# Token weights of a spectral mixer: transposed on TensorE in place of the DMA, with a new instruction order

## Chip, cores and metric

The kernel runs on one core of a Trainium2 chip. The metric is the device time of one execution in microseconds. Engines are named as in the profile: PE is TensorE (PEld its weight loads), DVE is VectorE, ACT is ScalarE, POOL is GpSimd, SP is the engine that issues all DMAs here.

## What is computed

Two stages follow each other for a batch of 4, sequence length 768. The first is attention of 8 heads of width 64 that looks only at selected chunks of 32 keys: an upper bound of each chunk's scores is formed from the minimum and maximum of its keys, and the six chunks with the highest bound are kept. The second mixes tokens and channels with a phase.

```python
ub = sum(maximum(q * k_min, q * k_max))            # per query and chunk
top_chunks = argsort(where(causal, ub, -1e9))[..., -6:]
scores = where(selected & causal, q @ k.T / 8, -1e9)
x = softmax(scores) @ v                            # heads joined: (4, 768, 512)

theta = x @ w_theta
zr, zi = x * cos(theta), x * sin(theta)
y = einsum('ts,bsd->btd', w_tok_r, zr) + einsum('ts,bsd->btd', w_tok_i, zi)
u = x + y
out = u + maximum(u @ w_ch, 0)
```

All inputs and the output are fp32; the kernel computes its large products in fp16 with fp32 accumulation.

## The kernel before

**Attention.** Heads are worked in pairs, four pairs in each batch. `Lk`, `Lq` and `Lv` load a pair's keys, queries and values. PE turns keys and queries (`Tk`, `Tq`, L230 for batch 0 and L433 for the others), ACT and DVE bring them from PSUM to SBUF as `kx` and `qT` (L169 is ACT's copy helper, L171 DVE's, L172 POOL's), and DVE reduces the keys to the minima and maxima of the chunks (`km`, L239 and L445). PE forms the bounds (`ub`, L277 and L482), DVE finds each query's sixth largest and makes a mask of it, which is copied into extra rows of the queries (L526). Scores `sc` come from L341/L349 or L554, ACT exponentiates them (L357, L560), POOL or DVE cut the triangle (L369, L570, L568), PE multiplies with the values (`av`, L401), and DVE normalizes into `x16` (L411, L412).

**Mixer.** For each batch: `x16` is transposed (`xT`, by PE at L598 with copies at L582/L583, or by DMA at L590 for batches 2 and 3), `th` (L608) gives theta, ACT takes sine and cosine (L615, L619), DVE or POOL form `zi` and `zr` (L623). For each of six tiles of 128 output tokens, twelve matmuls of 512 columns (L633, L635) accumulate `y`, with the transposed token weights `K.wtok` as the stationary operand; DVE adds x (`u`, L641). `u` is transposed (by DMA at L647 or PE at L654), multiplied with `w_ch` (`ch`, L662), and `ot` (L668) goes out by L672.

**Token weights.** `weights()` brings the two 768x768 matrices in 12 row blocks, named by `ri` (real or imaginary) and `tt` (six blocks of 128 rows). Each block is loaded (`Lwtok`, L697) into one of six buffers of class `ld`, cast to fp16 (`cwtok`, on ACT, DVE or POOL) into one of four buffers of class `st`, and transposed into `K.wtok` by a DMA that SP issues (`Twtok`, L702). The tile `t` of every batch's mixer needs the two blocks with `tt = t`.

**Order.** The program is first recorded as a list of operations (`op` for one engine, `alt` for several engines to choose from), each with a cost in ns that only an offline search used. A string `ORDER` fixes the order in which all of them are issued and, by a suffix `b` or `c`, the second or third alternative for the engine. Each engine runs its own instructions in that order, and buffers of a class are handed out in that order too. A number before the bar in the string is a count of idle matmuls of 512 columns at the start that keep PE running, and an entry `F5` is five of 128 columns.

**Buffers that matter here.** PSUM has two tiles of class `sc` of two banks each, one of class `av` and three of class `mi`; the last serves turns, bounds, theta, y and ch.

Of the kernel before, what the change touches and what calls it, by code (L numbers as in the profile page):

```python
# [11 lines left out]
FP16 = mybir.dt.float16  # L12
# [6 lines left out]
    "4 1 2 29 477b 380b 730b 3 28 31 30 0 21 58 5 57 9 476 10 F5 14 6 17 55 15 7 406 36 18 12b 16 32 20b 56 8b "  # L19
    "19 39 11 48 34 13b F19 41 33 44 42 85 23 37 45 75 38 47b 35b 40b 24 22 50 25 450 26 82 51 F10 71 27 68 83 "  # L20
    "52 72 176 109 173 177 69b 167 178 174 84 53 59 74 63 168 379 61 175 161 65 162 64 164 169 60 113 165 54 "
    "F6 170 163 67b 179 46 62b 66 77 166 171 43c 49c 202 76c 199 102 203 78 172 185 134 200 193 204 79 184 194 "
    "183 201 90 186 187 110 190 91 188 195 181 92 125 95 80 98 191 96b 189 196 115 114 81 86 99 93b 192 376 "
    "180 73b 70 87 209 197 375 88 225 401 103c 101b 402 213 198b 377 211 226 94 182 135 210 378 104 212 214 "
    "227 136 126 89b 228 105 222 215 229 106 265 127 116 223 219 230 207 107 266b 381 224 403 108 216 404 384 "
    "220 206 111 385 100 205 131 386 217 97 208 412 221 242 140 390 414 218 413 254 388b 233 255 231 405 389 "
    "232 243 256 239 416 391b 415 240 248 244 234 237 236 249 387b 241 235 245 238 383 267 250 246 251 268 407 "
    "451 729 252 269 247 410 128 411 270b 258 253 259 417b 257 409 112c 262 132 408 260 261 137 263 382 392 "
    "264 394 133 141 393 395 271 418 398b 397 272 142 420 396b 419b 278 129c 123 421b 138 283 280 130 423 298 "
    "424 139 293 299 282 300 273 301 149 295 119 427 152 274 124 158 275 276 146 428 284 155 437 288 294 277 "  # L30
    "279 286b 303 302 285 281b 310 289 297 304 287 150b 311 291b 296b 312 290 151 429 120 305 438 430 153b 317 "
    "318 292 422b 154 439 319 159b 320 431 321 440 147b 121 432 322 160 441 306 434c 323 307 442b 445c 444b "
    "308 443c 148 156b 436c 562 309 530 433c 563 349 435 313 157 331 332 122 333 117 531 564 543 143 314 399 "
    "350b 334 532 449 544 517 425 345 448 335 346 518 470 559 545b 338 560 519 339 118 340 341 561 447 144c "
    "342 446 315 145 549 316 343 550 556 400c 472 363 344 551 557 475 533 364 474 355 534 336 558b 356 347 546 "
    "337 348b 372 535b 547 365 357 373 473 426b 548 523 358 536 524 554 553 552 471b 353 525b 374 555 520 537 "
    "465 354 463 727 521 466b 538 540 457 452 726 464 461 522 539 469b 541 467 459b 324 453 542 325 728 458 "
    "326 456 327 359 460 526 527 455 496 328 454b 462b 329 468c 528 753 489 330 369 490 754 529 483 370 725 "
    "621 484 566 622b 371 565 486 567 478 485b 491 480 751 487 492 481 351 752 495b 494 360 482 479b 488b 749 "
    "493 352 742 361 366 743 568 362 498 367 497b 368 623 508 624 797 744 509 768 499 745 510 796 769 766 747 "  # L40
    "736 746b 767b 731 773 511 738 735 770 772b 795 512 733 739 514c 732 794 740 516c 513b 760 771b 515c 737b "
    "585 818 763 611 586 764 755 748 612 759 750 588 819 757b 587 762 734 608 821 589 613b 500 741b 820 758 "
    "761 582 590 609 501 765b 816 775 502 583 610 503 505c 506b 507b 584 756 774 601 785 776 504c 595 1070 602 "
    "786 777 1069 787 592 596 603 572 778 811 591 573 597 569 779 798 788 812 803 574 801 575 570 1068 827 780 "
    "593 1067 807 784c 576 598 594 783c 829 614 577 789 599 571 580 831 793c 579 830 615 792c 578 890 600 806 "
    "828 906 616 581 800 618 782c 907 617 790c 802 619 604 804 605 620 908 606 805 808b 887 799 607 822 891 "
    "625 817c 840 627 626 888 1089 893 628 1071 826 894 654 889 1073b 824 895 1074 903 823 791 656 898 825 900 "
    "1072b 634 832b 892b 781 1075 841 896 897 655 629 658 635 1091 657b 636 1092 899 639 637 630 644 631 638 "
    "632b 641 649 633 640 1090c 646 643 666 1134 642b 667 645 1135 648 668 651 647b 687 650 653 688 904 652 "
    "689 669 659 660 661 901 662 905b 663 690 902 670 909 664 877 665 691 878 867 701 692 868 911 879 880 693 "  # L50
    "910 881 869 861 705 912 671 862 882 874 672 809 875 833 863 810b 1113 835 864 702 834b 836 885 876b 815b "
    "707 813c 865 837c 1156 884 839 883 708 838 719 886 709 866 842 720 1114b 814c 871 721 872 852 1158 870 "
    "673 843 1159 674 853 873 680 681 854 1076 1157c 682 1077 1180 855 683 1078 1094 844 856 684 1093 845 685 "
    "858b 859c 857b 675 686 860b 932 958 846 933 1095 704 1079 676 1096 847 934 929 1097 1080 848c 677 959 "
    "1098 850c 678 930 1081b 1099 926 960 679 1100 927 1084 931 1101b 1137 1082 955 703 849 1083 851 928b 937 "
    "1085 1102b 916 956 1103 1086 716 1136 1104 1160 917 1087 935 1161 913 717 1108 957 914 1106 718 918 919 "
    "1105 1088 710 1109 1107b 915 920 1112 942 711 1110 936 943 1115 938 712 921 1111 694 1116 952 944 1125 "
    "1143 1117 953 1126 713 1118 1127 1144 939 1145 923 954b 940 945 1128 924 1119 695 1129 946 696 941 1146 "
    "697 1133c 1131b 1120 947 698 714 1124b 1132c 699 1123b 1122c 1147 922 715 1230 1121c 700 1240 1130c 1231 "
    "925 1151 706 1138 1152b 1162 1241 1232 1246 1139b 948 962 1141 1247 1242 1233 1164b 949 1140 1248 1243 "  # L60
    "1166 1234 961 1142 963 1244 950 1235 1227 964 1167 951 1228 1207 1245 1149 1170 1250 968 1208 1229 1171 "
    "1214 1150 1249 1148 1169b 1209 1204 1215 1154 969 1165 1175 1251 1163b 1168 1153 1201 1252 1205 966 1173 "
    "1216 722 1174b 1176 1172 1202 1206b 965 1237 1179 1236 723 1178 1238 1217 1177b 1239 1220 1203 724 991 "
    "1218 967 1155 1181c 1182 1221 1219 970 993 1222 1224 1192 1225 1223 1183 976 1226 992 971 1184 995 978 "
    "994b 1212 1185 977 981 973 980 1210 1186 972 1211 975 996 982 979b 974b 983 986 984b 998 1193 985 1187 "
    "1008 997 1000b 1194 1009 987 1015 988 1213 999 1016 1190b 1017 1191b 1010 1188b 990b 1022 1285 1279 1189c "
    "1286 1023 989b 1024 1195 1018 1196 1019 1200 1197c 1280 1011 1287 1259 1020 1198b 1281 1253 1260 1021 "
    "1025 1199b 1261 1256 1254 1045 1012 1001 1257 1255 1292 1002 1293 1258 1269 1263 1270 1264 1294 1282 1003 "
    "1283 1271 1262 1026 1265 1266 1284 1295 1267 1290 1289 1027 1296 1268 1272 1028 1288 1013 1273 1291 1297 "
    "1298 1046 1036 1299 1274b 1037 1014 1277 1300 1275 1276 1044 1301 1303 1278 1302 1004 1304 1005 1006 1309 "  # L70
    "1029 1007 1030 1031 1310 1032 1033 1034 1306 1058 1035 1038 1305 1059 1331 1055 1307 1333 1039 1056 1040 "
    "1060 1041 1308 1332 1316 1335 1042 1334 1057 1311 1318 1048 1317 1052 1320 1312 1319 1047 1321 1313 1053 "
    "1315 1326 1323 1314b 1043 1322 1336 1325 1327 1324b 1054 1348 1328 1329b 1349 1337 1330b 1341 1338 1342 "
    "1343 1340 1362 1339b 1350 1363 1364 1344 1345 1365 1366 1367 1351 1368 1352 1353 1386 1049 1354 1346 1050 "
    "1384 1061 1347 1355 1051 1062 1064 1383 1376 1065 1377 1063 1378 1066 1369 1370 1371 1372 1373 1374 1356 "
    "1375 1357 1358 1387 1359 1388 1360 1391 1361 1379 1392 1385 1403 1400 1393 1404 1380 1405 1401 1381 1394 "
    "1402 1382 1389 1397 1390 1395 1406 1398 1396 1407 1399 1408 "
)

B, H, S, D = 4, 8, 768, 64  # L80
P = 128
DM = H * D
NT = S // P
CH = 32
NCH = S // CH
QS = 192
NS = S - QS
# [3 lines left out]
NEG = -1000.0  # L91
KX = D + NCH
ROW = (0,)
X_DMA = (2, 3)
U_DMA = {(b, t) for b in (1, 2, 3) for t in range(NT) if b < 3 or t < 4}
SEGS = [(0, 4), (1, 3), (2, 5)]
BASE = [0, 1024, 2048]
# [61 lines left out]
def record(G):  # L159
# [515 lines left out]
    def weights():  # L675
# [12 lines left out]
        for tt in range(NT):  # L688
            for ri in range(2):
# [11 lines left out]
                def tr(ri=ri, tt=tt, a=a):  # L701
                    nc.sync.dma_start_transpose(out=K.wtok[:, :, ri, tt * P:(tt + 1) * P], in_=T(a))  # L702
# [193 lines left out]
```

## Time and profile before

| | |
|---|---|
| median of six executions | 240.2 us (238.96 to 242.02) |
| profiled execution | 238.96 us |
| its span, first to last instruction | 237.3 us |
| mean granted clock of PE | 0.982 |
| PE busy | 221.7 us, 93% |
| DVE busy | 174.8 us, 74% |
| ACT busy | 168.1 us, 71% |
| POOL busy | 93.6 us, 39% |
| DMA queue's share of 16 engines | 67.8%, in 106527 packets |

Busy time is the time from an instruction's start to its end, with overlapping ones counted once. Matmuls are pipelined, so consecutive ones start closer together than their own durations. An engine runs its queue in order: an instruction that waits holds all behind it. In a group's row, the number after `x` is a count, then come the sum of busy us and the mean ns of one, then the idle time just before them and what ended it. The profiled execution is one of the six, and the fastest of them.

### The profile page before, as it was taken

How to read it: one execution, taken by the hardware profiler on the slowest of the kernel's cores; microseconds unless marked ns; L12 is line 12 of the kernel's file. 1: busy time of each engine (PE TensorE's matmuls, PEld its weight loads, DVE VectorE, ACT ScalarE, POOL GpSimd, SP SyncE). 2: the span in 40 equal slices, each digit the busy share in tenths (PEclk: the TensorE clock that was granted, in tenths of full speed). 3: DMA queues.
4: the chain of work that ended last, by engine and by line, in shares of the span. 5: the costliest groups of instructions: out<-in, count | busy, mean ns of one | idle time of the engine just before them, and what ended most of it. 6: DMA issues, size and time to landing. Idle time of an engine off the chain costs nothing.

```text
span 237.3 us, 5648 instructions
## 1 busy us (share of the span) xinstructions
PE 221.7 (93%) x2086; PEld 126.6 (53%) x2086; DVE 174.8 (74%) x520; ACT 168.1 (71%) x251; POOL 93.6 (39%) x190
## 2 busy tenths in 40 slices
PE   7999998987999996899899999999899999999993
PEld 3755676533557554366445646657554564444441
DVE  3898998768167999699963998999988155445264
ACT  2559999997969358999996749789998970750000
POOL 8436665653232136456422404844607430320000
PEclk9999999999999999589999999999999999999998
DMA  7999998999999999842741698711620114642434
GB/s 161 268 246 267 288 205 260 228 252 261 262 276 272 262 270 280 184 94 53 161 95 25 140 257 144 196 48 32 112 61 0 22 25 88 162 106 40 159 118 171
DMA packets 106527, 38.85 MB, mean 164 GB/s; under 512 B 100620, under 2 KB 100748, under 8 KB 106500
## 3 DMA queue, kind: packets, MB, share of 16 engines
q1 hardware_dynamic: 106500, 38.50, 67.8%
q8 instruction: 16, 0.26, 0.4%
q14 instruction: 11, 0.09, 0.1%
HBM read 26.17 MB, written 6.29 MB: 137 GB/s over the span
## 4 chain that ended last, share of the span: by engine, by line
PE 59%; ACT 18%; DVE 15%; issue 3%; DMA 3%; SPq 0%; POOL 0%; ACTq 0%; DVEq 0%
PE y L633 9%; PE y L635 9%; PE sc L554 7%; PE th L608 7%; ACT pt L560 7%; PE ch L662 6%; PE av L401 4%; ACT kx L169 4%; ACT pt L357 3%; PE ub L482 3%; DMA wtok<-in_moe_w_tok_i_dram 3%; DVE km L445 3%; PE qps L433 2%; DVE kx L171 2%; PE sc L341 2%
## 5 line engine op out<-in xcount | busy, mean ns | idle before, releaser
L560 ACT ACTIVATE pt<-sc 128x1024 f16<-128x1024 f32 (+1 forms) x72 | 62.8, 925 | 8.2 <-PE sc L554 7.6
L633 PE MATMUL y<-zr,wtokT 128*128 128x512 f16 x144 | 54.6, 379 | 0.0
L635 PE MATMUL y<-zi,wtokT 128*128 128x512 f16 x144 | 54.5, 379 | 0.0
L554 PE MATMUL sc<-qx,kx 88*128 88x512 f16 (+3 forms) x192 | 39.6, 317 | 5.7 <-POOL qx L526 2.0
L570 POOL TENSOR_SCALAR_AFFINE_SELECT pt<-pt 128x256 f16<-128x256 f16 x60 | 25.1, 421 | 42.7 <-ACT pt L560 42.0
L401 PEld LDWEIGHTS <-pt 128*128 128x128 f16 x672 | 27.0, 98 | 8.6 <-issue 1.6
L401 PE MATMUL av<-v,pt 128*128 128x65 f16 x672 | 30.6, 194 | 0.7 <-ACT pt L357 0.5
L641 DVE TENSOR_TENSOR u<-y,x 128x512 f16<-128x512 f32 x24 | 16.5, 686 | 19.2 <-PE y L635 19.1
L554 PEld LDWEIGHTS <-kx 88*128 88x128 f16 x192 | 17.2, 99 | 24.4 <-issue 7.2
L445 DVE TENSOR_REDUCE km<-kps 128x12 f32<-128x384 f32 x48 | 24.9, 545 | 2.3 <-PE kps L433 1.1
L662 PE MATMUL ch<-wch,uT 128*128 128x512 f16 x96 | 24.1, 379 | 0.0
L608 PE MATMUL th<-wtheta,xT 128*128 128x512 f16 x96 | 22.7, 379 | 1.3 <-DVE ubT L498 0.6
L357 ACT ACTIVATE pt<-sc 128x1024 f16<-128x1024 f32 (+1 forms) x24 | 21.0, 921 | 1.3 <-PE sc L349 1.1
L633 PEld LDWEIGHTS <-wtokT 128*128 128x128 f16 x144 | 14.0, 97 | 14.6 <-issue 0.7
L635 PEld LDWEIGHTS <-wtokT 128*128 128x128 f16 x144 | 14.1, 98 | 14.0 <-issue 0.3
L172 POOL CAST qx<-qT 64x768 f16<-64x768 f32 (+1 forms) x21 | 15.9, 764 | 14.0 <-ACT qT L169 11.5
L169 ACT COPY qT<-qps 128x384 f32<-128x384 f32 x21 | 9.9, 491 | 14.3 <-PE qps L230 8.7
L668 DVE SCALAR_TENSOR_TENSOR ot<-ch,u 128x512 f32<-128x512 f32 x24 | 16.3, 685 | 4.9 <-PE ch L662 4.9
L169 ACT CAST kx<-kps 64x384 f16<-64x384 f32 (+1 forms) x34 | 15.8, 472 | 4.7 <-PE kps L433 4.3
L412 DVE TENSOR_TENSOR x<-av,rec 128x384 f16<-128x384 f32 x32 | 17.8, 558 | 1.1
L619 ACT ACTIVATE cs<-th,pi 128x512 f16<-128x512 f32 x24 | 16.5, 700 | 1.1 <-PE th L608 1.0
L526 POOL COPY qx<-nsT 24x288 f16<-24x288 f16 x26 | 11.0, 424 | 12.3 <-DVE nsT L518 11.2
(94 smaller groups left out, 351.0 us busy)
## 6 DMA issues: line engine op xcount, KB each, us to landing
q<-in_q_dram SPq DMA_DIRECT2D x32, 192.0 KB, 3.3
k<-in_k_dram SPq DMA_DIRECT2D x32, 192.0 KB, 3.4
v<-in_v_dram SPq DMA_DIRECT2D x16, 384.0 KB, 4.0
out_dram<-ot SPq DMA_DIRECT2D x24, 256.0 KB, 2.3
wtok<-in_moe_w_tok_i_dram SPq DMA_DIRECT2D x6, 384.0 KB, 5.3
wtok<-in_moe_w_tok_r_dram SPq DMA_DIRECT2D x6, 384.0 KB, 4.6
wth<-in_moe_w_theta_dram SPq DMA_DIRECT2D x4, 256.0 KB, 3.8
wch<-in_moe_w_ch_dram SPq DMA_DIRECT2D x4, 256.0 KB, 3.2
```

Source lines behind the costliest of these rows:

```text
L169: c = {"A": ("ACT", int(n * 0.833 + 60), 0, lambda: nc.scalar.copy(out=out(), in_=in_())), "D": ("DVE", int(n / 0.96 + 70) if psum else in ...
L357: nc.scalar.activation(out=T(pt)[:, :, base:base + w], in_=T(ps).rearrange("p (x c) -> p x c", x=2)[:, :, 0:w], func=AF.Exp, bias=0.0, sca ...
L401: nc.tensor.matmul(ps[:, t, :], T(pt)[:, x, o:o + P], T(v16)[:, x, j, :], start=(j == 0), stop=(j == t))
L412: nc.vector.tensor_tensor(out=T(x16)[:, :, h * D:(h + 1) * D], in0=ps[:, :, 0:D], in1=T(rec).broadcast_to([P, NT, D]), op=ALU.mult)
L445: nc.vector.tensor_reduce(out=T(km)[:, j, 12 * f:12 * f + 12], in_=T(ps)[:, 0:384].rearrange("p (c w) -> p c w", w=CH), axis=AX.X, op=o)
L554: nc.tensor.matmul(T(ps)[:, a0:a1], T(kx)[0:KX, x, j * P:(j + 1) * P], T(qx)[0:KX, x, q0 + a0 - o:q0 + a1 - o], start=True, stop=True)
L560: nc.scalar.activation(out=T(pt)[:, x, BASE[s]:BASE[s] + w], in_=T(ps)[:, 0:w], func=AF.Exp, bias=0.0, scale=SCALE)
L570: eng.affine_select(out=a, in_=a, pattern=[[0, 2], [1, P]], compare_op=ALU.is_ge, fill=G.zero_reg(), base=0, channel_multiplier=-1)
L608: nc.tensor.matmul(T(ps), T(xT[t])[:, c, :] if by_dma else T(xT[c])[:, t * P:(t + 1) * P], K.wtheta[:, c, :], start=(c == 0), stop=(c == 3))
L633: nc.tensor.matmul(T(ps), K.wtok[:, si, 0, t * P:(t + 1) * P], T(zr[si]), start=(si == 0), stop=False)
L635: nc.tensor.matmul(T(ps), K.wtok[:, si, 1, t * P:(t + 1) * P], T(zi[si]), start=False, stop=(si == NT - 1))
L662: nc.tensor.matmul(T(ps), T(uT[t])[:, c * P:(c + 1) * P], K.wch[:, c, :], start=(c == 0), stop=(c == 3))
```

## The change

Each of the 12 fp16 row blocks is transposed on PE: six transposes of 128x128 (`Tw`) into one PSUM tile of class `mi`, and one copy (`evw`), on DVE or ACT, from there into `K.wtok`. A set `W_DMA` names the blocks that would still go by DMA, and it is empty. The offline costs of the DMA transposes of `x` and `u` are lowered from 900 to 750, which only the search sees. The string `ORDER` is replaced as a whole: order, choices of engines and idle matmuls (ten of 512 columns as before; 42 of 128 columns where there were 40). Evictions `evw` stand nine times on DVE and three times on ACT. Other choices of engine that moved: casts of values (ACT 4 to 2, DVE 8 to 2, POOL 4 to 12), casts of token weights (ACT 5 to 2, DVE 2 to 1, POOL 5 to 9), casts of queries (ACT 6 to 1, DVE 5 to 4, POOL 21 to 27), copies of keys (ACT 34 to 39, DVE 22 to 17) and of queries (ACT 21 to 16, DVE 11 to 16).

```diff
 ORDER = (
     "10|"
-    "4 1 2 29 477b 380b 730b 3 28 31 30 0 21 58 5 57 9 476 10 F5 14 6 17 55 15 7 406 36 18 12b 16 32 20b 56 8b "
...
+    "4 1 3 2 742b 28 29 30 31 0 21 55 14 56 17 15b 9 417 18b 5 20b 7 57 418 11 F10 36 19 32 10 58 16 35 6 463 "
...
 X_DMA = (2, 3)
+W_DMA = ()
...
-                   lambda t=t: nc.sync.dma_start_transpose(out=T(xT[t]), in_=T(x16)[:, t, :]), dma=900)
+                   lambda t=t: nc.sync.dma_start_transpose(out=T(xT[t]), in_=T(x16)[:, t, :]), dma=750)
...
-                   dma=900)
+                   dma=750)
...
-                def tr(ri=ri, tt=tt, a=a):
-                    nc.sync.dma_start_transpose(out=K.wtok[:, :, ri, tt * P:(tt + 1) * P], in_=T(a))
-                op("SP", f"Twtok.{ri}.{tt}", 1270, [(a, 0)], [("wtok", (ri, tt))], tr, dma=1200)
+                def wt(ri=ri, tt=tt):
+                    return K.wtok[:, :, ri, tt * P:(tt + 1) * P]
+                if tt in W_DMA:
+                    op("SP", f"Twtok.{ri}.{tt}", 1270, [(a, 0)], [("wtok", (ri, tt))],
+                       lambda a=a, wt=wt: nc.sync.dma_start_transpose(out=wt(), in_=T(a)), dma=1100)
+                    continue
+                ps = buf("mi", f"wps.{ri}.{tt}", (S,), FP16)
+
+                def tr(a=a, ps=ps):
+                    for c in range(NT):
+                        nc.tensor.transpose(T(ps)[:, c * P:(c + 1) * P], T(a)[:, c * P:(c + 1) * P], K.ident16)
+                op("PE", f"Tw.{ri}.{tt}", 330, [(a, 0)], [(ps, 0)], tr)
+                alt(f"evw.{ri}.{tt}",
+                    [("DVE", 470, 0, lambda ps=ps, wt=wt: nc.vector.tensor_copy(out=wt(), in_=T(ps).rearrange("p (c t) -> p c t", t=P))),
+                     ("ACT", 705, 0, lambda ps=ps, wt=wt: nc.scalar.copy(out=wt(), in_=T(ps).rearrange("p (c t) -> p c t", t=P)))],
+                    [(ps, 0)], [("wtok", (ri, tt))])
```

## The prediction

> **What bounds the kernel now.** I read the slices of the span first, then stage windows, then the chain. In the page's slices a digit is the tenth of a slice of 5.9 us that an engine was busy.
>
> ```profile
> PE   7999998987999996899899999999899999999993
> DVE  3898998768167999699963998999988155445264
> ACT  2559999997969358999996749789998970750000
> PEclk9999999999999999589999999999999999999998
> DMA  7999998999999999842741698711620114642434
> ```
>
> PE is busy nearly throughout, and DMA is full for the first 16 slices, 95 us. But busy counts a matmul's latency, so I also took PE's work from the timeline: the spacing of starts of each form of matmul (0.215 us for 512 columns, 0.055 for 128 in fp16; pairs side by side at half) times its count. That gives 200.8 us of work. The first matmul starts at 1.3 us and the last at 233.0, so gaps take 31.0 us: 10.0 up to 44 us, 2.8 from 48 to 64, 9.3 from 80 to 104, 3.6 from 104 to 120, 5.0 after. The windows (engines' busy us, then granted clock, DMA share, GB/s) say what stands there:
>
> ```profile
> 48.00:64.00 16.00, 13.91 (x98) 6.30 (x97) 9.02 (x38) 14.21 (x22) 6.51 (x12) 1.00 1.04 253
> 64.00:80.00 16.00, 16.00 (x150) 9.79 (x148) 11.85 (x26) 11.82 (x17) 4.20 (x9) 1.00 1.16 276
> 80.00:88.00 8.00, 7.43 (x89) 4.47 (x95) 7.84 (x17) 4.59 (x8) 1.89 (x4) 1.00 1.07 261
> 88.00:96.00 8.00, 5.36 (x58) 3.21 (x38) 7.24 (x26) 6.12 (x11) 4.04 (x7) 0.97 1.14 282
> 96.00:104.00 8.00, 7.57 (x70) 3.65 (x69) 6.22 (x39) 7.46 (x12) 4.20 (x11) 0.61 0.65 149
> ```
>
> From 64 to 80 PE is full (batch 0's mixer) while DVE and ACT have 4 us spare each; right after it DVE, then ACT, are full and PE stands. The chain of waits shows where a weight load is in it (start, us, what):
>
> ```profile
> 50.48 6.89 DMA wtok<-in_moe_w_tok_i_dram
> 57.37 0.02 issue
> 57.39 0.04 ACTq L169
> 57.42 0.04 issue
> 57.47 0.83 ACT wtok L169
> 58.30 0.02 issue
> 58.32 0.43 ACT qx L526
> ```
>
> ACT, in order, waits for a token weight's load, and behind it stands the mask copy L526 for which the scores L554 wait.
>
> **What the Trainium skill says.** "VectorE: DVE Perf Modes", section "The three transpose paths", gives 390 ns for a 128x128 on TensorE, into PSUM, and 1309 ns by DMA. Here six transposes on PE ran in 0.51 us together; a DMA transpose of 128x768 held SP's queue for 1.235 us and landed after 3.5. The order of the two agrees. "DMA: Bandwidth & Descriptors", section "Specifications", wants transfers of at least 512 B for line rate; the page of before counts 100620 of 106527 packets under that. "TensorE: Matmul & The Clock Gate", Part 1, says that a window of some 3.4 us with PE idle halves its clock; PEclk falls to 0.61 in the window from 96 us, after PE's emptiest one, which agrees.
>
> **The change, part by part.** Prices for what is added:
>
> ```profile
> 82.40 0.51 PE L598 MATMUL xps<-ident,x 128*128 128x128 f16 x6
> L582 DVE COPY xT<-xps 128x768 f16<-128x768 f16 x5 | 2.7, 548 | 0.8 <-PE xps L598 0.8
> L583 ACT COPY xT<-xps 128x768 f16<-128x768 f16 x3 | 2.4, 799 | 0.2 <-PE xps L598 0.2
> L702 SPq DMA_TRANSPOSE wtokT<-wtok x12: 1210/1235/1472, 29.6 to 70.0; - x12
> ```
>
> *Added on PE:* 12 x 6 transposes at 0.055 us = 4.0 us. These are the shape of L598, so price and form are known. PE is the engine that sets the end, so they count in full, except where PE would stand anyway; that is in the gap count below.
>
> *Added on DVE and ACT:* the built order puts nine evictions on DVE (9 x 0.548 = 4.9 us) and three on ACT (3 x 0.799 = 2.4). The same order takes casts off them: of v, DVE 8 to 2 and ACT 4 to 2; of wtok, ACT 5 to 2 and DVE 2 to 1; POOL gets these (v 4 to 12, wtok 5 to 9). POOL has the room: 93.6 us busy, some 17 more. Net for DVE and ACT is -2 to -3 us each, so I cost the evictions at nothing on their sums; if POOL's casts come late, the 7.3 us return. The evictions wait for PE in DVE's and ACT's queues, in front of reductions and exponentials, and each turn holds one of three small PSUM buffers for PE's 0.51 us and the copy; with PE, not they, late this costs nothing, and up to 12 x 0.55 = 6.6 us if PE must wait for a buffer each time. I take zero.
>
> *Removed:* 12 DMA transposes. On SP 12 x 1.235 = 14.8 us of queue, and waits: L702 is among SP's waits, up to 2.0 us at once (for ACT cs). Loads that stood behind them move forward. On the DMA engines each is 768 packets of 256 B at 19.4 ns (the trace's mean for this size) over 16 engines = 0.93 us, 11.2 us in all, within the 95 us that are full. Ordered by issue, batch 1's last keys come after 76 us of DMA work in the old order and 62 in the new, batch 2's first after 85 and 68, though PE reaches their use 2.5 and 1 us of its own work later. So data stops being what sets 48 to 104 us.
>
> *The wait at 50 us:* goes with the ACT casts moved and the loads earlier. What is late next is ACT or DVE. Of the 2.8 us I take 2.3; ends 0 and 2.8.
>
> *The reordering:* I counted, in both built orders, the work of each engine placed beside every 5 us of PE work (each instruction at its row's mean; rows overlap, so DVE's and ACT's sums are scaled to their busy totals, by 0.91 and 0.90). Where DVE or ACT has more than 5 us beside 5 of PE, PE must stand unless queues absorb it. Excess, before and after, by position in PE's own work: 0 to 35, 7.2 and 6.9; 35 to 70, 2.9 and 0.2; 70 to 90, 8.9 and 8.8; beyond, 6.0 and 2.1. Sum 25.0 and 18.0. The old sum lies under the measured 31.0 gaps, in the same places, so I trust its differences. The 15 us of PE work from position 75 still carry 23.0 us of DVE (the old cluster, from 70: 22.1 of ACT, 21.7 of DVE), so I expect the empty stretch near 80 to 104 us to stay, clock dip included. The difference is -7.0 us, with the 2.3 us of the wait inside it; ends -2 (only that wait) and -10.5 (the clock dip goes too: 6.8 us at half clock, 3.4 us).
>
> *Sum:* 237.3 + 4.0 - 7.0 = 234.3 us of span. The profiled execution took 238.96, 1.7 over its span, and is the fastest of six; their median 240.2 is 1.2 higher. So 236.0 for such an execution, 237.2 for the median, -1.25%.
>
> **Rivals.**
>
> *The dip goes as well.* With loads 14 us earlier in DMA work, PE's gaps near 90 us spread out and no idle window halves the clock: -3.4 more, 233.8. For: DMA is full until 96 us and k lands only 3.5 us after issue, just ahead of use. Against: the DVE cluster is as dense as before.
>
> *It cancels.* Only the one weight wait goes, and of the later smoothing about half a microsecond is real, because the gaps after 104 us are latencies between engines and not excess: 237.3 + 4.0 - 2.3 - 0.5 = 238.5, median 241.4; with half of the later smoothing, 239.7. I take 240.4. For: ACT, at 7.5 to 7.9 of 8 us from 24 to 48 us, gets no relief there.
>
> *Slower: PE waits for the weights itself.* Before, a late weight held SP and, once, ACT; PE only at the mixer. Now each of the 12 transposes stands in PE's in-order queue before the mixer, from position 21 on, and everything behind it waits. The weight turned at position 36 needs 11.6 MB loaded; the windows of before had moved as much by 48 us, and PE was at position 37 at 51.0 us. With 0.8 us for the cast the margin is some 1 us. A wtok load landed in 2.7 to 7.4 us, median 4.0; one at the long end costs 3.4. With half of the later smoothing lost: 237.3 + 4.0 + 3.4 - 2.3 - 2.0 = 240.4, median 243.3. It ends over 1% slower once PE's lateness passes 2.7 us.
>
> That the change doesn't do what it says is excluded: the built order has the 72 transposes on PE and no L702.
>
> **How the numbers follow.** Forecast 0.50 (237.2, its own range 235 to 239.5), dip gone 0.14, cancels 0.20, slower 0.16. About 1%, 2.4 us, is what a measurement of this kernel can tell from no change. Faster by over 1% (under 237.8): 0.42 of the forecast and all of the dip case, 0.56. Within: 0.08 and 0.17, 0.25. Slower (over 242.6): 0.03 of the cancelling case and all of the slower, 0.19. Leaving out the outer part of the dip case and most of the slower gives a range of 232.0 to 242.4.
>
> **What would show it.** Right: PE's work 4 us up; no DMA in the chain near 50 us; PE windows full from 48 to about 80 us; gaps after 110 us about half; DMA share under 1 before 90 us. A clock dip near 90 to 105 us keeps the forecast, its absence the first rival. Wrong: PE's new transposes listed as waiting for casts of wtok or for its DMAs, with the first mixer matmul later than 55 us (51.0 now, plus the 4); or gaps after 104 us that stay at 8.6 us.

## The result, and the profile after

Median of the changed kernel 238.36 us in 29 runs, against 240.08 us in 66 runs of the kernel before: ratio 0.9942, 95% interval 0.9925 to 0.9960, so 1.4 us (0.6%) by the ratio. That is a gain, smaller than the 1% that one measurement of this kernel can tell from nothing. The forecast was 237.2, a gain of 1.25%, so the kernel gained less than half of what was forecast, though the time lies inside the forecast's own range of 235 to 239.5. The profiled execution took 238.04 us with a span of 236.0, where the prediction's sum gave 236.0 with a span of 234.3.

PE's work and gaps, in us, taken from the trace as the prediction took them (spacing of starts times count; what is left between starts is a gap). The last four columns give the gaps by position in PE's own work: position 35 is the place where PE has done 35 us of it. Which spacing is taken for a form, and on which side of a boundary a wait falls, moves a single entry by up to 1 us.

| | span | PE's work | gaps | 0 to 35 | 35 to 70 | 70 to 90 | from 90 |
|---|---|---|---|---|---|---|---|
| before | 237.3 | 200.7 | 31.2 | 11.0 | 5.0 | 10.1 | 5.1 |
| after | 236.0 | 204.8 | 26.0 | 11.9 | 0.9 | 8.9 | 4.3 |
| after, a second time | 235.8 | 204.8 | 25.9 | 11.2 | 1.4 | 8.9 | 4.4 |

Work went up by 4.1 us and gaps fell by 5.2, which leaves 1.1 of the 1.3 us of span. The page's slices of the changed kernel (tenths busy, 5.9 us each):

```profile
PE   7999998999999998788989999999999999999993
DVE  3898899989455699999995888897988444354453
ACT  2559989798595677999989179799989960660000
PEclk9999999999999999999999999999999999999999
DMA  7989999897962789990830167902440113560553
```

DMA is no longer full throughout the first 95 us, and PEclk has no dip any more. Still PE's digits fall to 7 and 8 in the slices from 94 us, where DVE and ACT show 9. The windows of the changed kernel say the same (PE, weight loads, DVE, ACT, POOL busy, then clock, DMA share, GB/s):

```profile
48.00:64.00 16.00, 15.33 (x113) 7.38 (x113) 12.75 (x46) 12.37 (x21) 8.42 (x13) 1.00 0.99 256
64.00:80.00 16.00, 16.00 (x123) 9.85 (x122) 9.35 (x18) 12.01 (x16) 5.01 (x10) 1.00 0.47 117
80.00:88.00 8.00, 8.00 (x82) 5.29 (x81) 5.99 (x14) 5.40 (x12) 4.85 (x9) 1.00 0.97 243
88.00:96.00 8.00, 6.37 (x98) 4.26 (x95) 7.90 (x28) 6.22 (x12) 2.92 (x6) 1.00 1.05 265
96.00:104.00 8.00, 6.46 (x63) 3.70 (x63) 7.26 (x42) 7.82 (x15) 5.60 (x12) 1.00 1.01 228
```

PE is busy for 15.33 of 16 us from 48 (13.91 before) and throughout 64 to 88, but from 88 to 104 DVE and ACT in turn have no room and PE stands: its gaps there are 6.6 us, and were 7.6 with the clock dip. The wait at 50 us has gone. PE's waits between 20 and 64 us had this row before the change:

```profile
PE sc L554 <- ACT qx L526: 1.4, 1, 1.4
```

After the change, the longest in that stretch are these:

```profile
PE kps L434 <- DMA k<-in_k_dram: 0.5, 1, 0.5
PE sc L342 <- ACT pt L358: 0.5, 2, 0.3
PE ub L483 <- DVE wtokT L715: 0.3, 1, 0.3
```

No score waits for a mask copy behind a late weight, and none of PE's turns there has a listed wait for a cast. The tile view of `wps` shows who waits for them:

```profile
L712 PE MATMUL wps<-ident,wtok x72: 216/219/221, 30.8 to 70.8; 128*128 128x128 f16 x72
  ACT wtokT L716: 2.2, 2
  PEld ub L483: 0.9, 1
```

ACT's queue stood for 2.2 us at two of its three copies because PE came late, and the weight load of a bound (`PEld ub`) waited 0.9 us once for such a copy to free its PSUM buffer.

### The profile page after: what moved, and what is told of

Its sections match the earlier page's. It is cut to its first block, busy times and chain, and to the rows that moved or that the text cites. A ratio compares the mean times of both kernels' runs of the same rounds, so it can differ in the third digit from the quotient of the medians.

```text
span 236.0 us, 5784 instructions
## 1 busy us (share of the span) xinstructions
PE 222.7 (94%) x2160; PEld 130.8 (55%) x2160; DVE 175.8 (75%) x518; ACT 165.7 (70%) x246; POOL 110.9 (47%) x209
## 4 chain that ended last, share of the span: by engine, by line
PE 65%; DVE 15%; ACT 11%; issue 3%; DMA 2%; POOL 2%; SPq 0%; POOLq 0%; DVEq 0%; ACTq 0%
PE y L634 12%; PE y L636 12%; PE ch L663 8%; PE sc L555 7%; PE th L609 5%; PE av L402 4%; ACT pt L561 4%; ACT kx L170 3%; ACT pt L358 3%; PE ub L483 2%; DMA k<-in_k_dram 2%; DVE x L413 2%; PE kps L434 2%; PE warm L834 2%; DVE km L446 2%
## 5 line engine op out<-in xcount | busy, mean ns | idle before, releaser
L571 POOL TENSOR_SCALAR_AFFINE_SELECT pt<-pt 128x256 f16<-128x256 f16 x58 | 23.6, 412 | 33.5 <-ACT pt L561 32.2
L555 PE MATMUL sc<-qx,kx 88*128 88x512 f16 (+3 forms) x192 | 37.4, 305 | 1.9 <-ACT pt L561 1.5
L173 POOL CAST qx<-qT 64x768 f16<-64x768 f32 (+1 forms) x27 | 20.8, 778 | 10.4 <-ACT qT L170 4.9
L669 DVE SCALAR_TENSOR_TENSOR ot<-ch,u 128x512 f32<-128x512 f32 x24 | 16.5, 689 | 10.1 <-PE ch L663 9.8
L170 ACT CAST kx<-kps 64x384 f16<-64x384 f32 (+1 forms) x39 | 18.2, 476 | 7.9 <-PE kps L231 3.0
L609 PE MATMUL th<-wtheta,xT 128*128 128x512 f16 x96 | 23.3, 379 | 0.0
L527 POOL COPY qx<-nsT 24x288 f16<-24x288 f16 x28 | 12.3, 440 | 18.8 <-DVE nsT L519 16.7
L624 POOL TENSOR_TENSOR zi<-x,sn 128x512 f16<-128x512 f16 x8 | 10.1, 1273 | 14.3 <-ACT sn L616 14.1
```

What stands on the lines that cost most here:

```text
L170: c = {"A": ("ACT", int(n * 0.833 + 60), 0, lambda: nc.scalar.copy(out=out(), in_=in_())), "D": ("DVE", int(n / 0.96 + 70) if psum else in ...
L555: nc.tensor.matmul(T(ps)[:, a0:a1], T(kx)[0:KX, x, j * P:(j + 1) * P], T(qx)[0:KX, x, q0 + a0 - o:q0 + a1 - o], start=True, stop=True)
L571: eng.affine_select(out=a, in_=a, pattern=[[0, 2], [1, P]], compare_op=ALU.is_ge, fill=G.zero_reg(), base=0, channel_multiplier=-1)
L609: nc.tensor.matmul(T(ps), T(xT[t])[:, c, :] if by_dma else T(xT[c])[:, t * P:(t + 1) * P], K.wtheta[:, c, :], start=(c == 0), stop=(c == 3))
```

## The experiments

### Without any transposition

In both orders, the cast writes straight into the transposed tile, and the transposition (with its copy, in the new order) is left out, so the token weights stand untransposed and the output is not the right one; only the time is of use.

```diff
-copies(..., [(a, 0)], lambda: T(a), ...)        # then Twtok, or Tw and evw
+copies(..., [("wtok", (ri, tt))], lambda ri=ri, tt=tt: K.wtok[:, :, ri, tt*P:(tt+1)*P], ...)
```

> Old order without any transposition of the token weights: the casts write their row block straight into the weights' place, so the 12 blocks stand untransposed; loads, casts and all else stay. The ceiling of what taking 12 DMA transposes away is worth in the old order. Theory 1 (the old order itself, not DMA time, sets most gaps): 1 to 2.5 us under before. Theory 2 (DMA time sets the stretch from 48 to 104 us): 5 us or more under before, with most of the 9.3 us of gaps from 80 to 104 us gone. Theory 3 (transfers are hidden anyway): within 0.7 us of before.

> New order without transposition of the token weights (row blocks stand untransposed as in the run above): the 72 transposes on PE and the 12 copies are gone. Theory 1 (PE sets the end, its added work counts in full): 4.0 us under the changed kernel, 5.5 under before. Theory 2 (transposes and copies also add waits in front of the mixer): 6 us or more under the changed kernel. Theory 3 (the work lies partly in gaps that stay): 1 to 3 us under the changed kernel.

The old order without transpositions took 237.27 us, ratio 0.9898 [0.9864, 0.9931]; the new order 236.35, 0.9875 [0.9819, 0.9931]. So taking the twelve DMA transposes away, with no other instruction reordered, is worth about 1.0% or 2.4 us (0.7% to 1.4%). Gaps at positions 35 to 70 fall from 5.0 to 3.4 us, and the score's wait of 1.4 us for a mask copy is no longer among PE's waits; everything else stays, the stretch of 80 to 104 us above all (windows of the old order without transpositions):

```profile
48.00:64.00 16.00, 15.28 (x107) 7.16 (x107) 10.14 (x41) 15.51 (x24) 6.51 (x14) 1.00 0.83 229
88.00:96.00 8.00, 4.97 (x30) 2.96 (x30) 7.70 (x27) 7.80 (x14) 4.41 (x8) 0.93 1.04 238
96.00:104.00 8.00, 7.90 (x76) 4.50 (x76) 5.70 (x38) 7.31 (x12) 4.27 (x10) 0.64 0.50 115
```

The queue and the DMA engines are relieved, the DMA share from 48 us is 0.83 where it was 1.04, and yet PE has only 4.97 us of 8 from 88, gaps of 7.4 us from 88 to 104, and the same dip. The twelve transposes set the wait at 50 us; they did not set what follows 80 us. The DMA share from 88 us is still 1.04 in this kernel, but neither here nor in the kernel before does any engine's listed wait from 86 to 104 us end with a transfer.

The other comparison prices PE's turns. The new order with them took 0.9942, without them 0.9875: 1.6 us at the centres, 2.0 us of span in the traces, for 4.0 us of PE's work and twelve copies. The intervals just overlap, so by them the size is only known to lie between some 0.2 and 3 us. The two were not timed side by side, either: a second series of the changed kernel, below, gave 0.9909, and against that one the turns cost 0.8 us. Between the two orders, both without transpositions, the difference (0.9898 and 0.9875) is not resolved. Read together: relief of DMA about -2.4 us, the order perhaps -0.6, the turns +0.8 to +1.6.

### One part alone

The old order with PE turns: the code after the change with the old `ORDER`, each `Twtok` replaced by `Tw` and `evw`. Each `Tw` stands behind its cast, just ahead of the next PE operation at which a small PSUM buffer is free, up to some 30 entries later than its `Twtok` had stood. The new order with DMA transposes: `W_DMA` full, each `Twtok` put where its cast is done. In both, these places were chosen by hand from a trace; no others were tried.

```diff
-W_DMA = ()
+W_DMA = (0, 1, 2, 3, 4, 5)      # new order; the other kernel keeps () with the old ORDER
```

> Old order, transposes on PE: each DMA transpose is replaced by six transposes on PE and a copy, put where the trace of before shows its cast done (just ahead of the next PE operation with a free small PSUM buffer), copies on the engines that the changed kernel uses. Theory 1 (the gain needs the new order): 1 to 4 us over before. Theory 2 (turning on PE is the gain, the order little): 1 to 2 us under before.

> New order, DMA transposes: the 12 transposes go back to SP, each put where the trace of the changed kernel shows its cast done. Theory 1 (the new order is the gain and PE's 4.0 us are a loss): 2 to 4 us under the changed kernel. Theory 2 (the new order works only with the DMA queue relieved): 1 us or more over the changed kernel, its loads late from 40 to 80 us.

Old order with PE turns: 246.72 us, 1.0296 [1.0249, 1.0343]. New order with DMA transposes: 246.07, 1.0267 [1.0217, 1.0317]. Each part alone, so placed, loses near 3% (6.5 us by the ratio), more than the 1 to 4 us that were expected of the first. In the first, turns land among the selection of keys and the mixer. The chain of the old order with PE turns (start, us, what):

```profile
55.14 0.72 ACT wtok L169
55.87 0.60 ACT cs L619
56.51 0.51 PE wps L711 x6
57.04 0.56 DVE wtokT L714
57.68 0.68 DVE t L509 x9
```

The turn at 56.51 us waits for ACT's `cs`, a reader of the small PSUM buffers, and that `cs` stands behind a cast of the weights in ACT's queue; the copy then takes its place in DVE's queue ahead of `t`, a step of the selection of keys. The tile view of `wps` in the same kernel:

```profile
  DVE wtokT L714: 5.0, 8
  ACT wtokT L715: 1.3, 2
```

DVE waited 5.0 us for PE's turns, in eight of its nine copies; in the new order DVE waited 0.2. That agrees with the Trainium skill, "PSUM — Partial Sum Buffer", section "Engine vs sequencer instructions", which calls the queues of ACT, DVE and POOL strictly first in, first out: a copy that waits for PE stops what is behind it. PE's work is 4.0 us more and its gaps 3.7 us more than before (31.2 to 34.9).

In the second, the mixer waits for DMA. The chain of the new order with DMA transposes:

```profile
39.49 7.12 DMA wtokT<-wtok
48.92 5.19 DMA wtok<-in_moe_w_tok_r_dram
54.18 0.83 ACT wtok L168
60.30 3.98 DMA wtokT<-wtok
64.32 0.61 PE y L632
```

The mixer's first two matmuls start at 58.6 us (55.1 in the changed kernel), then PE waits 5.0 us for a DMA transpose and goes on at 64.3. PE's gaps up to position 35 are 23.7 us (11.9 in the changed kernel). Neither the turns without the new order nor the new order without the turns gained anything; whether a better placing would keep part of the gain is not shown.

### The clock dip

Eight idle matmuls of 512 columns ahead of one score group put work into PE's hole at 92 us of the kernel before.

```diff
+if (b, h, s) == (1, 5, 1):
+    for _ in range(8):
+        nc.tensor.matmul(T(ps)[:, 0:512], K.zero[:, 0:P], K.zero, start=True, stop=True)
```

> Kernel before with eight idle matmuls of 512 columns (1.7 us) in the hole from 91.9 to 93.9 us in which PE waits for a mask copy; they write the scores' tile ahead of the scores themselves. PE has work in that window, so its clock should not drop to half from 95.5 to 102.3 us. Theory 1 (the dip is real cost, as rival 'dip goes as well' had it): 2 to 3.4 us under before. Theory 2 (DVE and ACT set that stretch and hide the dip): within 1 us of before.

239.39 us, 0.9979 [0.9952, 1.0007]. The windows:

```profile
88.00:96.00 8.00, 7.09 (x66) 4.09 (x51) 7.25 (x25) 5.97 (x11) 3.89 (x7) 1.00 1.15 284
96.00:104.00 8.00, 6.66 (x70) 3.88 (x69) 6.50 (x41) 7.61 (x12) 4.47 (x11) 0.79 0.70 160
```

In this trace the dip shrank from 6.8 to 3.4 us (mean clock from 96 us: 0.79, was 0.61), which at half of its length lost is worth 1.7 us; the interval allows 1.2 at most. The other executions say more. The mean clock of PE over the span had a median of 0.998 in them, and 0.983 in those of the kernel before beside them: 12 of the 22 stood at 0.997 or more and had hardly any dip left. By these medians some 3.6 us of full clock came back, and the time fell by no more than that 1.2 us. PE at full speed simply stood for longer (6.66 us busy, was 7.57), while DVE and ACT did the same work. The changed kernel says it again: no dip, and gaps of 6.6 us from 88 to 104 us where they were 7.6. This holds for the one dip that lies where DVE and ACT are full. Of the executions of the kernel before that enter the comparisons, the 25 with a mean clock under 0.98 had spans of 239.3 us in the median and the 114 others 237.7; no trace of such an execution was kept, so whether a further dip made them longer, or longer waits made the dip, stays open.

### Half of each order

The new order up to its 736th entry (some 110 us) and the old from there, and the reverse, were to tell which half holds the gain; then the same with the seam near 93 us.

```diff
-ORDER = new
+ORDER = new[:736] + [op for op in old if op not in new[:736]]    # second pair: 609
```

> New order, with transposes on PE, up to PE's position 83 (110 us); from there the remaining operations in the old order. If the count of excess is right, which gave the new order 3.9 us of its gain past position 90: about 4 us over the changed kernel. If the gaps measured there are right (5.1 before, 4.3 after): 0 to 1.5 us over the changed kernel, some of it from the seam of two orders.

> Old order, with DMA transposes, up to PE's position 83 (111 us); from there the remaining operations in the new order. By the count of excess: 3.9 us under before. By the measured gaps: 0.9 us under before at most, less the seam.

> New order with transposes on PE up to PE's position 70 (93 us), the rest in the old order. By the measured gaps (4.1 us more work and 3.2 less gap up to 70, 2.1 less gap after it) it should stand 2.1 us over the changed kernel, about 0.4 over before. By the count of excess (2.9 less gap up to 70, 4.0 after): 4.0 over the changed kernel.

> Old order with DMA transposes up to PE's position 70 (91 us), the rest in the new order. By the measured gaps: 2.1 us under before. By the count of excess: 4.0 under before. If the new rest needs loads that the old head has not yet issued: no gain.

| | median, ratio to before | gaps | 0 to 35 | 35 to 70 | 70 to 90 | from 90 |
|---|---|---|---|---|---|---|
| new head, seam 110 us | 242.82, 1.0134 [1.0107, 1.0160] | 29.9 | 10.4 | 1.6 | 12.8 | 5.0 |
| old head, seam 110 us | 240.74, 1.0021 [0.9989, 1.0053] | 32.6 | 11.6 | 5.5 | 12.2 | 3.2 |
| new head, seam 93 us | 242.30, 1.0102 [1.0069, 1.0134] | 30.1 | 11.1 | 1.0 | 13.0 | 5.0 |
| old head, seam 93 us | 244.87, 1.0195 [1.0137, 1.0254] | 36.8 | 10.8 | 8.2 | 14.8 | 3.1 |

All four put 2 to 5 us into positions 70 to 90, where the seams lie, more than the differences that they were to find. The windows of the new head with the seam at 110 us show what a seam looks like:

```profile
104.00:112.00 8.00, 5.10 (x66) 3.43 (x63) 6.40 (x16) 6.89 (x10) 4.71 (x13) 1.00 0.23 53
112.00:120.00 8.00, 7.65 (x77) 5.13 (x77) 5.02 (x11) 5.60 (x7) 3.75 (x9) 0.79 0.01 2
```

From 104 us no engine is full, and DMA is nearly empty. Probably the work that the new order would have begun there is not yet due in the old order's list. In the old head with the seam at 93 us it is a transfer:

```profile
96.00:104.00 8.00, 1.82 (x8) 0.94 (x9) 4.44 (x19) 5.33 (x11) 2.96 (x6) 0.65 1.09 247
```

PE is busy for 1.82 us in 8, no compute engine is full, and the DMA share is 1.09; a load of values that takes 4.1 us from 95.8 us is in the chain, with ACT's cast and copies of keys behind it. What these runs do say, past the seam: the new order's tail has gaps of 3.1 to 3.2 us past position 90 where the old one's has 5.0, so it is worth 1.9 us at most, wherever it follows the old head. That half of the order alone carries the gain is not shown by any of them.

### Where PE's turns cost

Two of the twelve turns come late, at 69.0 and 70.5 us, where PE has no gap. In the next kernel these two blocks go by DMA; in another a third does too; in another all the other ten are turned twice, with `W_DMA` empty.

```diff
-W_DMA = ()
+W_DMA = ((0, 4), (1, 5))        # with three blocks: (0, 3) as well
...
-if tt in W_DMA:
+if (ri, tt) in W_DMA:
...
-    for c in range(NT):
+    for c in 2 * list(range(NT)) if (ri, tt) not in ((0, 4), (1, 5)) else range(NT):   # turned twice
```

> Changed kernel with two of the 12 blocks (imaginary 5 and real 4, turned by PE at 69.0 and 70.5 us, where PE has no gap and the DMA share is 0.47) transposed by DMA at 59 us. PE work falls by 0.66 us and two copies leave DVE or ACT. Theory 1 (PE sets this stretch, so work taken from it counts in full): 0.7 us under the changed kernel. Theory 2 (the gaps near 90 us take it up again): no difference. A loss of more than 0.5 us would say that SP's queue, held 2.4 us longer at 59 us, delays keys and queries.

> Changed kernel with the six transposes of ten of the twelve row blocks done twice over (the two that PE turns at 69.0 and 70.5 us stay single): 60 more transposes, 3.3 us more PE work, between 31 and 62 us, with nothing more on DVE, ACT, SP or the DMA. If PE's added work counts in full, as the prediction had it: 3.3 us over the changed kernel. If it lies in gaps that DVE and ACT leave there anyway, as the run without transposes suggests: 0.3 to 1.3 us over.

> Changed kernel with three blocks by DMA: the two of the run with two, and real 3, which PE turns at 62.1 us. PE work falls by 1.0 us. If PE is full there: 0.3 us under the kernel with two by DMA, 1.2 under the changed kernel. If the transpose, issued at 58 us and needed at 63.5, comes late: over the kernel with two.

Two by DMA: 237.24 us, 0.9909 [0.9881, 0.9938]. Turned twice: 238.88, 0.9984 [0.9961, 1.0007]. Three by DMA: 238.81, 0.9952 [0.9926, 0.9977].

Sixty more transposes are 3.3 us more of PE's work (208.1 us in the trace), and cost 1.0 us against the changed kernel's 0.9942 (0.3 to 1.7 by the intervals), or 1.8 against the second series' 0.9909: 0.3 to 0.5 us for each us of turns. Gaps fall from 26.0 to 23.4 us, most of it in the first 64 us, where PE has gaps to fill. The tile view of `wps`, turned twice:

```profile
L711 PE MATMUL wps<-ident,wtok x132: 217/219/221, 30.4 to 71.7; 128*128 128x128 f16 x132
  ACT wtokT L715: 2.8, 3
  DVE wtokT L714: 1.2, 3
```

The copies wait 4.0 us for PE now, where they waited 2.4. The two late turns may be another matter: 0.67 us of PE's work, and about 0.8 us gained by moving them to the DMA engines, whose share there was only 0.47. The interval of this difference runs from nothing to 1.6 us; two further comparisons follow. With the third block the gain is gone; its profiled execution has a gap of 3.9 us at 64 to 80 us, but at a span of 239.9 us that one is slower than its median, so the place is not certain.

### The key load in the chain

The changed kernel's chain has a load of keys in it that was not in the old one's:

```profile
26.33 0.43 SPq L180
26.80 5.46 DMA k<-in_k_dram
32.40 0.52 PE kps L434 x3
```

On SP, this load and its neighbour were exchanged with a weight's load ahead of them, in the changed kernel and in the one with two blocks by DMA.

```diff
 # order on SP
-Lwtok.0.1 ... Lk.1.0.1 Lk.1.0.0
+Lk.1.0.1 Lk.1.0.0 ... Lwtok.0.1
```

> Changed kernel with the loads of batch 1's first keys and of token weight block real 1 exchanged on SP. The chain of the changed kernel holds 5.46 us of that key load, and PE waits 0.5 us for it at 32.4 us. Theory 1 (the chain's load is worth its wait): 0.5 us under the changed kernel. Theory 2 (DVE and ACT are full there, the item in the chain is worth nothing): within 0.3 us.

> Two blocks by DMA and the early key load together. If both are worth something, they add: 1.3 us under the changed kernel. If the key load is worth nothing, as with two blocks alone: 0.8 to 1.1 under the changed kernel.

238.16 us, 0.9936 [0.9912, 0.9960], and with two blocks by DMA 237.91, 0.9946 [0.9921, 0.9971]. Against the changed kernel's 0.9942 neither adds anything. In this pair, timed together, moving two blocks to DMA gained nothing either, where 0.8 to 1.3 us were expected of the two edits together. A chain item of 5.46 us was worth nothing that shows: PE's own wait for it was only 0.5 us. What takes its place was not followed further.

### The best of them once more

The changed kernel and the one with two blocks by DMA, both as they were, were run side by side.

> The changed kernel again, beside the runs of this group on the same chip. 0.58% under before, as measured; it is the base for the three others.

> Two blocks by DMA, again. If PE's work from 64 to 80 us counts in full: 0.7 us under the changed kernel of this group. If its first comparison was a lucky one: within 0.3 us of it.

237.84 us, 0.9909 [0.9875, 0.9942], and 237.09, 0.9875 [0.9832, 0.9917]. Two blocks by DMA are 0.75 us (0.3%) below the changed kernel here and were 0.8 us (0.3%) below it before; the intervals of each pair overlap. Sign and size agree in these two, and the third comparison, with the early key load, shows no gain, so the 0.3% is likely and not shown. It has the lowest ratio of all complete kernels tried. What differs between the two series of the changed kernel, 0.9942 and 0.9909, stays open; their intervals overlap.

## Why the prediction was off

**PE's added work**, +4.0 us: measured 4.1 (200.7 to 204.8). The sum let each turn count in full and left what falls into gaps to the count of excess. The runs give the share: removing turns and copies together gains 2.0 us of span, and doubling ten turns costs 1.0 to 1.8 us for 3.3. Half of the 4 us or more lies in gaps.

**The copies at nothing**: not quite. Three of them stand in the changed kernel's chain between 40 and 49 us, on DVE, of which this is the last:

```profile
48.43 0.48 DVE wtokT L715
48.95 1.20 PE ub L483 x30
```

At 0.3 to 0.5 us for each us of turns, an estimate from the doubled turns, the 4.0 us would cost 1.2 to 2.2; removing turns and copies gained 2.0 of span. So the copies cost between nothing and some 0.8 us; they were never taken away alone. The wait for a small PSUM buffer, taken as zero, shows once, as the 0.9 us of `PEld ub`.

**The removed DMA and the wait at 50 us**: right for 48 to 80 us. The wait is gone, PE is full from 64 to 88 us, and gaps between positions 35 and 70 fell by 4.1 us, more than the 2.7 forecast. Loads come earlier, as the DMA share of 0.47 from 64 us suggests. It was wrong that data set anything from 80 to 104 us: with the transposes simply removed, that stretch is unchanged. The windows had said so, since DVE and then ACT were full there.

**The reordering**, -7.0 us: this is the step that failed. The gaps fell by 5.2 us, and not where the count of excess had put it:

| position in PE's work | change of excess, forecast | change of gaps, measured |
|---|---|---|
| 0 to 35 | -0.3 | +0.9 |
| 35 to 70 | -2.7 | -4.1 |
| 70 to 90 | -0.1 | -1.2 |
| from 90 | -3.9 | -0.8 |
| sum | -7.0 | -5.2 |

The tail, which was to give more than half, gave a fifth of that; the middle gave more than forecast, so the sum came nearer than its parts by luck. The order's own share is smaller still. From the kernel before, gaps fell by 1.5 us with the DMA transposes gone (31.2 to 29.7), by 1.7 with the new order in addition (to 28.0), and by 2.0 because PE's turns fill gaps (to 26.0). Between the two kernels without transposition, where PE's work is the same and only the order with its choices of engines differs, the count gives -6.9 and the gaps -1.7. So the forecast's +4.0 for the turns and its -7.0 were both too large, in opposite directions: by the spans the turns cost 2.0, the order gained 1.6 and the removed DMA 1.7.

The sentence that carried the count was that the old sum lay under the measured gaps in the same places, so its differences could be trusted. In the tail it did not: beyond position 90, which the kernel before passes near 119 us, the old excess was 6.0, and the prediction had measured 5.0 us of gaps after 120 us. Nor does the count stand still when its 5 us stretches are moved. Worked out again from both orders and traces, with the prediction's two scales, it gives higher levels (33.7 before, 26.2 after) and a difference of -7.5; with all stretches begun 1, 2, 3 or 4 us later, the difference is -0.9, -6.7, -6.4 or -5.0.

With the kernels above the count can be asked directly. As the prediction took it, it gives for them (it sees the order alone and no transfer):

| | excess | measured gaps | gaps less excess |
|---|---|---|---|
| before | 25.0 | 31.2 | 6.2 |
| old order, no transposition | 25.0 | 29.7 | 4.7 |
| after | 17.9 | 26.0 | 8.1 |
| new order, no transposition | 18.1 | 28.0 | 9.9 |
| new order, DMA transposes | 18.1 | 38.6 | 20.5 |
| old head, seam 110 us | 18.4 | 32.6 | 14.2 |
| new head, seam 110 us | 19.0 | 29.9 | 10.9 |
| old head, seam 93 us | 20.9 | 36.8 | 15.9 |
| old order, PE turns | 22.5 | 34.9 | 12.4 |

The excess does not rank them. Kernels with 18 to 19 us of excess have gaps from 26.0 to 38.6 us, and the two with the most, 25.0, stand in the middle with 29.7 and 31.2. What the count leaves out, 5 to 20 us, moves by more than the count itself. For the tail the rival "it cancels" had offered a reason: gaps after 104 us are latencies between engines, not excess. It is not shown by an experiment, but the changed kernel's waits between 104 and 136 us carry two such rows, of one and the same place:

```profile
PEld L402 <- DVE x L413: 1.3, 1, 1.3
PE av L402 <- DVE x L413: 0.8, 1, 0.8
```

Here one head's product waits for the normalisation `x` in DVE's queue. After 104 us the gaps fell from 8.7 to 6.6 us, where about half had been named as the sign of being right.

**The clock dip**: it vanished, as the first rival had it, and brought nothing that shows of its 3.4 us; putting the clock back in the kernel before gained 1.2 us at most. The Trainium skill, "TensorE: Matmul & The Clock Gate", Part 1, counts half of the throttled time as lost; in this case that price was too high, most likely because DVE and ACT set those 16 us. The agreement that the prediction saw with that page, an idle window of some 3.4 us ahead of the dip, is loose: the longest stretch without a matmul there was 2.04 us, from 91.89 us, and with it filled a dip of 3.4 us still came at 98.5 us.

**From the sum to the median**: the sum was for a profiled execution, 236.0, and 1.2 us were added because the kernel before lay that far under its median. The changed one's lies 0.3 under its own, which covered part of the miss by chance: 2.0 us off for the profiled execution, 1.2 for the median.

**The slower rival**: PE waits for no weight, and the mixer starts at 55.1 us, within 0.1 of the limit that the prediction named. The mechanism exists, though: in the new order with DMA transposes PE waits 5.0 us for one weight.

## What to carry to other kernels

A sum of busy times per stretch of an order can say where an engine has no room, not what a different order is worth. Before a difference of such sums is used, it should reproduce the gaps of two orders that have already been measured, stretch by stretch, and it should stay when the stretches are cut elsewhere. Work added to the engine that sets the end is cheap where that engine has gaps (0.3 to 0.5 us for one here); where it has none, it may cost in full (some 0.8 us for 0.67, in two comparisons of three). A change of order and a change of means belong together when the order was made for the means: in this case half of either, taken back by hand, measured the seam.

## What the runs showed of the hardware

Raising PE's mean clock from 0.983 to 0.998 by filling a hole in its work gained 0.2%, and at most 0.5%, with DVE and ACT full beside it. Twelve DMA transposes of 128x768 held back a kernel of 240 us by 1.0% (0.7% to 1.4%), and most of the gap that went with them lay at a single wait. Six fp16 transposes on PE take 0.50 us together, and turning ten blocks twice, 60 transposes more, cost a third to a half of the time that they add to PE's work.
